# Three copies of the first y on two engines, and one softmax piece moved behind an output sum, in a fused dynamic convolution and squared-ReLU FFN

## Chip, cores and metric

One core of a Trainium2 chip. The metric is device time of one execution in microseconds (us). The program runs on one core, so there is no other core to compare with, and every profiled run here had a mean granted TensorE clock of 1.000. The "span" of a trace, from the first to the last instruction, is some 1.7 us shorter than the device time of the same execution (746.6 for 748.35).

## The reference

```python
# x: 8 x 4096 x 192, weight_gen: 8 x 4096 x 8 heads x 7 taps
w = softmax(weight_gen, axis=-1)
out[b, s, h, g] = sum over k of w[b, s, h, k] * x_pad[b, s + k, h, g]   # six zeros ahead of each sequence
h = np.maximum(out.reshape(32768, 192) @ w_in, 0.0)                     # 192 x 2048
return (h * h @ w_out).astype(np.float32)                               # 2048 x 192
```

## The kernel before

The tokens are cut into blocks: two of 512, then 31 of 1024. A block of 1024 has 16 units (the first two blocks have eight) and is followed, in the next block, by the eight parts of its second matmul. The prediction and the text below call each of these parts a quarter and count them from 1 to 8 in the block in which they run; the code counts two of them as one. A convolution of the next block stands near the end of every block. TensorE does the convolution as matmuls with banded matrices; VectorE builds the bands from the softmax rows.

The convolution writes PSUM tiles `yp`, and ScalarE copies them to `y`. For the first blocks, with 512 tokens, one tile holds all three chunks of 256 columns:

```python
def st_conv(j):
    th = BLOCKS[j][1] * TB // 2            # 256 columns for j == 0
    per = 1024 // th
    yps = [ps_h.tile([P, 2 * TB], f32, name="yp", tag="h") for _ in range(-(-NK // per))]
    # ... banded matmuls into yps ...
    for n, yp in enumerate(yps):
        k0, k1 = n * per, min((n + 1) * per, NK)
        nc.scalar.copy(
            out=y[:, k0:k1, 0:th],
            in_=yp[:, 0 : (k1 - k0) * th].rearrange("p (k c) -> p k c", c=th),
        )
```

A unit (`st_unit`, "u") is a set of matmuls into `h`, ScalarE's Relu of 1024 columns into `t` and VectorE's square into `g`. A quarter ("M") of a block of 1024 is 32 matmuls into two PSUM accumulators with one buffer each. Every second M ends with the output sum:

```python
def o_sum(j, qt, ccs, o):
    # ...
    nc.scalar.copy(out=o_sb, in_=o[0][:, c])
    if len(o) == 2:
        nc.vector.tensor_tensor(out=o_sb, in0=o[1][:, c], in1=o_sb, op=AluOp.add)
```

The next quarter into the same accumulators waits for that sum (in the trace of before once for long enough to be listed, 0.62 us). Softmax is done in parts and pieces: ScalarE takes the exponential of a piece ("E"), VectorE does the rest ("S"):

```python
def soft(s):
    lo, hi = next(s.softs)
    s.total(lo, hi)
    s.recip(lo, hi)
    s.scale(lo, hi, nc.vector)
    # ... after the last piece of a part: send the rows off by DMA
```

The order is written by hand for blocks 0 to 3 and from tables after that ("B": bands, "C": convolution, "L": load of raw weights):

```python
steady = "MuMuuu" * 3 + "MuuuMCu"
plans = {
    # ... blocks 0 to 2 ...
    3: "L5 L6 M S3 u u u M u u u u M u M B6 E4 u u u M M B7 u u S4 u E4 M u C M u",
}
TIMES = {(1, 0): ((3, 15), (4, 0)), (1, 1): ((4, 15), (5, 0)), ...}   # (block, unit) of each piece
us = {6: (7, 9)}.get(j, (5, 9) if small else (1, 5))                  # units ahead of which the bands stand
```

The softmax here doesn't subtract the row's maximum and nothing guards it: scores larger than these inputs give would overflow.

## Time and profile before

| | before |
|---|---|
| device time, median of 3 | 748.11 us (747.69 to 749.93) |
| span in the trace | 746.6 us |
| TensorE, VectorE, ScalarE busy | 99%, 83%, 84% |
| wait for the first y | 0.9 us, once |
| wait for an output sum | 0.6 us, once, near 78 us |

Busy shares say how near an engine is to full over the whole span; the two waits are what the change is aimed at. They add up to 0.2% of the time, so the question is one of tenths of a microsecond, read from the starts of instructions. The lines stand in the prediction below.

### The profile page before, as it was taken

What the parts mean: (1) busy time and instruction counts of PE and PEld (TensorE: products, weight loads), DVE (VectorE), ACT (ScalarE), POOL (GpSimd) and SP (SyncE); (2) the same over time, 40 slices, a digit from 0 to 9 for tenths busy, and PEclk for the clock granted to TensorE, in tenths of its full rate; (3) what the DMA queues carried; (4) which work ended last, traced back from release to release, by engine and by line L of the source; (5) the groups of instructions that cost most, each with busy time, mean ns of one, the idle gap of its engine ahead of it and who ended that gap; (6) DMA issues with size and microseconds to landing.
All of it is one profiled execution on the core that took longest, in us unless ns stands there. A gap on an engine that the chain in (4) does not pass through costs nothing.

```text
span 746.6 us, 33289 instructions
## 1 busy us (share of the span) xinstructions
PE 739.0 (99%) x15106; PEld 556.5 (75%) x15106; DVE 621.8 (83%) x1001; ACT 624.7 (84%) x755; POOL 88.8 (12%) x130
## 2 busy tenths in 40 slices
PE   8999999999999999999999999999999999999998
PEld 4767877877777777777777777787777777777787
DVE  5999998998889888888889888898888987677853
ACT  5998788888888888888888888888888888888874
POOL 7321220101101100011000110001100011001000
PEclk9999999999999999999999999999999999999999
DMA  8654454436554234644245542365441354441312
GB/s 223 112 106 109 80 101 85 100 70 139 94 118 79 75 57 80 140 79 73 45 74 139 102 65 53 51 139 108 59 80 48 57 108 80 60 73 51 51 46 65
DMA packets 122169, 64.81 MB, mean 87 GB/s; under 512 B 83849, under 2 KB 118636, under 8 KB 121516
## 3 DMA queue, kind: packets, MB, share of 16 engines
q1 hardware_dynamic: 77708, 45.66, 22.4%
q0 software_dynamic: 44176, 16.93, 20.5%
q8 instruction: 118, 1.93, 1.1%
q14 instruction: 23, 0.19, 0.1%
q10 hardware_dynamic: 144, 0.10, 0.0%
HBM read 48.61 MB, written 28.70 MB: 104 GB/s over the span
## 4 chain that ended last, share of the span: by engine, by line
PE 94%; DVE 2%; issue 1%; DMA 1%; ACT 1%; POOL 0%; DVEq 0%; ACTq 0%
PE o L475 45%; PE h L441 43%; PE yp L416 6%; DVE g L453 1%; DVE bd L348 1%; DMA wr<-v_first 0%; DMA wg<-in_weight_gen_dram 0%; POOL wr L330 0%; ACT t L450 0%; DVE v_first L239 0%; ACT ex L217 0%; DVE ssum L224 0%; DVE rcp L231 0%; DVE o_sb L491 0%; ACT y L427 0%
## 5 line engine op out<-in xcount | busy, mean ns | idle before, releaser
L450 ACT ACTIVATE t<-h 128x1024 f16<-128x1024 f32 x512 | 496.7, 1026 | 65.6 <-PE h L441 65.3
L453 DVE TENSOR_TENSOR g<-t 128x1024 f16<-128x1024 f16 x512 | 334.3, 687 | 100.5 <-ACT t L450 97.8
L475 PEld LDWEIGHTS <-g 64*128 64x128 f16 (+1 forms) x8032 | 352.3, 94 | 55.0 <-issue 4.8
L475 PE MATMUL o<-w_o,g 64*128 64x192 f16 (+1 forms) x8032 | 385.3, 243 | 0.9 <-DVE o_sb L491 0.6
L441 PE MATMUL h<-y,w_i 64*128 64x512 f16 (+1 forms) x3168 | 379.7, 370 | 2.2 <-ACT t L450 0.9
L441 PEld LDWEIGHTS <-w_i 64*128 64x128 f16 x3168 | 162.6, 94 | 117.2 <-issue 5.2
L348 DVE TENSOR_TENSOR bd<-wr,mask 128x4160 f16<-128x4160 f16 (+3 forms) x89 | 149.3, 1701 | 4.0 <-DMA wr<-v_first 4.0
L300 POOL DMA_DIRECT2D xt<-in_x_dram x62 | 51.2, 830 | 446.7 <-PE yp L416 423.7
L489 ACT COPY o_sb<-o 128x384 f32<-128x384 f32 x129 | 62.2, 482 | 33.8 <-PE o L475 33.8
L491 DVE TENSOR_TENSOR o_sb<-o,o_sb 128x384 f32<-128x384 f32 x123 | 68.2, 555 | 8.4 <-ACT o_sb L489 5.6
L427 ACT CAST y<-yp 128x1024 f16<-128x1024 f32 (+1 forms) x64 | 48.1, 803 | 14.5 <-PE yp L416 14.5
L416 PE MATMUL yp<-bd,xt 128*32 128x104 f16 (+8 forms) x3864 | 51.7, 208 | 0.3 <-DVE bd L348 0.2
L416 PEld LDWEIGHTS <-xt 128*32 128x32 f16 (+3 forms) x3864 | 46.2, 92 | 6.7 <-issue 6.2
L239 DVE TENSOR_TENSOR v_big<-ex,rcp 128x112 f16<-128x112 f32 (+1 forms) x136 | 27.3, 263 | 1.8 <-DMA vd<-v_big 0.6
L217 ACT ACTIVATE ex<-wg 128x448 f32<-128x448 f32 (+2 forms) x44 | 27.2, 618 | 1.8 <-DMA wg<-in_weight_gen_dram 1.8
L224 DVE TENSOR_REDUCE ssum<-ex 128x64 f32<-128x448 f32 (+2 forms) x44 | 26.1, 594 | 2.5 <-ACT ex L217 2.3
L231 DVE RECIPROCAL rcp<-ssum 128x64 f32<-128x64 f32 (+2 forms) x44 | 23.7, 539 | 1.5
L290 POOL DMA_DIRECT2D xt<-in_x_dram x7 | 3.8, 549 | 135.8 <-PE yp L416 135.8
L330 POOL DMA_DIRECT2D wr<-v_first x31 | 16.8, 561 | 16.3 <-DVE v_first L239 16.1
L539 PE MATMUL wp<-warm 128*128 128x512 f16 x39 | 11.4, 459 | 1.3 <-DVE warm L531 1.3
L539 PEld LDWEIGHTS <-warm 128*128 128x128 f16 x39 | 4.3, 114 | 7.6 <-issue 3.5
L239 DVE TENSOR_TENSOR v_first<-ex,rcp 128x112 f16<-128x112 f32 (+1 forms) x48 | 9.1, 255 | 0.3
(24 smaller groups left out, 28.2 us busy)
## 6 DMA issues: line engine op xcount, KB each, us to landing
out_dram<-o_sb SPq DMA_DIRECT2D x63, 384.0 KB, 3.0
xt<-in_x_dram POOLq DMA_DIRECT2D x42, 240.0 KB, 5.9
wg<-in_weight_gen_dram SPq DMA_DIRECT2D x4, 1064.0 KB, 8.3
xt<-in_x_dram POOLq DMA_DIRECT2D x20, 192.0 KB, 5.6
wr<-vd SPq DMA_DIRECT2D x38, 80.0 KB, 3.6
vd<-v_big SPq DMA_DIRECT2D x5, 512.0 KB, 5.5
wg<-in_weight_gen_dram SPq DMA_DIRECT2D x5, 392.0 KB
wg<-in_weight_gen_dram SPq DMA_DIRECT2D x3, 616.0 KB, 4.1
```

The source lines that it names most:

```text
L217: nc.scalar.activation(out=self.ex[:, lo:hi].rearrange("p r g k e -> p (r g) k e"), in_=self.wg[:, lo:hi].rearrange("p r (g e) k -> p (r g ...
L239: eng.tensor_tensor(out=bass.AP(tensor=v.tensor, offset=v.offset + lo * H * SL + lo % SL * 2 + g * SL * 2, ap=[list(v.ap[0]), [H * SL + 2, ...
L300: eng.dma_start(out=dst[:, first:last], in_=ap)
L348: nc.vector.tensor_tensor(out=bd_t[j][:, H * lo : H * (lo + len(tiles) * n)].rearrange("p (g m c) -> p g m c", g=shape[1], c=2 * SL), in0= ...
L416: nc.tensor.matmul(out=yps[k // per][p0 : p0 + m, col + a : col + b], lhsT=x_t[s][:, i, 32 * q : 32 * q + m], rhs=bd[:, h // 2, h % 2, a - ...
L427: nc.scalar.copy(out=y[:, k0:k1, 0:th], in_=yp[:, 0 : (k1 - k0) * th].rearrange("p (k c) -> p k c", c=th),)
L441: nc.tensor.matmul(out=h[:, half, jj * th : (jj + 1) * th], lhsT=w_in_chunk(u * per + jj, slot, half), rhs=y_t[j][r0 : r0 + RT, k, 0:th], ...
L450: nc.scalar.activation(out=t1, in_=h, func=ActF.Relu)
L453: nc.vector.tensor_tensor(out=g, in0=t1, in1=t1, op=AluOp.mult)
L475: nc.tensor.matmul(out=oo[:, cc * Dm : (cc + 1) * Dm], lhsT=g[r0 : r0 + n, cc * P : (cc + 1) * P], rhs=w_o[r0 : r0 + n, fc, :], start=(fc ...
L489: nc.scalar.copy(out=o_sb, in_=o[0][:, c])
L491: nc.vector.tensor_tensor(out=o_sb, in0=o[1][:, c], in1=o_sb, op=AluOp.add)
```

## The change

Its intent: the first copy of y lies between the first convolution and the first unit, with nothing else for TensorE to do; three copies on two engines could be done sooner than one of 768 columns. And near 78 us an output sum comes late because a softmax piece stands ahead of it on VectorE; the piece goes behind the last output sum of block 3. What followed it (the second piece of that part, and the bands that need its rows) moves later too.

```diff
@@ st_conv
-            nc.scalar.copy(
-                out=y[:, k0:k1, 0:th],
-                in_=yp[:, 0 : (k1 - k0) * th].rearrange("p (k c) -> p k c", c=th),
-            )
+            copies = ((k0, k1, nc.scalar.copy),)
+            if j == 0:
+                copies = ((0, 1, nc.scalar.copy),) + tuple(
+                    (k, k + 1, nc.vector.tensor_copy) for k in range(1, NK)
+                )
+            for a, b, copy in copies:
+                copy(
+                    out=y[:, a:b, 0:th],
+                    in_=yp[:, (a - k0) * th : (b - k0) * th].rearrange("p (k c) -> p k c", c=th),
+                )
@@ plans
-            3: "L5 L6 M S3 u u u M u u u u M u M B6 E4 u u u M M B7 u u S4 u E4 M u C M u",
+            3: "L5 L6 M S3 u u u M u u u u M u M B6 E4 u u u M M B7 u u u M u M C S4 u",
@@ TIMES
-            (1, 0): ((3, 15), (4, 0)),
+            (1, 0): ((3, 15), (4, 1)),
-            (1, 2): ((4, 1), (5, 1), (5, 15)),
+            (1, 2): ((4, 2), (5, 1), (5, 15)),
@@ exp_time
-            return j, {1: 0, 7: 3, 9: 4, 15: 8}[u]
+            return j, {1: 0, 2: 1, 7: 3, 9: 4, 15: 8}[u]
@@ bands
-            us = {6: (7, 9)}.get(j, (5, 9) if small else (1, 5))
+            us = {4: (7, 9), 6: (7, 9)}.get(j, (5, 9) if small else (1, 5))
```

In the prediction and below, part 1 is the first y, part 2 the end of block 3, part 3 the second softmax piece, part 4 the bands.

## The prediction

> **What bounds the kernel now.** I read the page's busy table first, then the list of waits of TensorE, then the timeline around each of those waits. The busy table says that TensorE is never free for long:
>
> ```profile
> PE 739.0 (99%) x15106; PEld 556.5 (75%) x15106; DVE 621.8 (83%) x1001; ACT 624.7 (84%) x755; POOL 88.8 (12%) x130
> ```
>
> TensorE is busy for 739.0 of 746.6 us, so everything that any change of waits could win is under 8 us, or 1%. VectorE and ScalarE are at 83% and 84%: close enough to full that work moved from one place to another in their queues can come late somewhere else. Of TensorE's waits, all under 2 us, three matter here:
>
> ```profile
> PE h L441 <- ACT t L450: 0.9, 1, 0.9
> PE h L441 <- ACT y L427: 0.9, 1, 0.9
> PE o L475 <- DVE o_sb L491: 0.6, 1, 0.6
> ```
>
> Columns: waiter, what it waited for, total us, times, longest. The second is the wait for the first y, which the first part of the change is aimed at. The third is the wait for an output sum, which the second part is aimed at. Here is the first, in the timeline (start us, us, engine, line, operation):
>
> ```profile
> 14.70 0.80 ACT L427 CAST y<-yp 128x768 f16<-128x768 f32 x1 [1.92 <-PE yp L416]
> ...
> 14.89 2.36 DVE L348 TENSOR_TENSOR bd<-wr,mask 128x3328 f16<-128x3328 f16 x2 [0.73 <-DMA wr<-v_first]
> ...
> 15.55 2.80 PE L441 MATMUL h<-y,w_i 64*128 64x256 f16 x48 [0.89 <-ACT y L427]
> ```
>
> The reader sees one ScalarE copy of 0.80 us between the convolution and the first unit, 0.05 us of signalling after it, and VectorE starting the bands of block 1 at 14.89. The other wait, on TensorE:
>
> ```profile
> 76.85 0.81 PE L441 MATMUL h<-y,w_i 64*128 64x512 f16 x6
> 77.57 0.24 PE L475 MATMUL o<-w_o,g 64*128 64x192 f16 x1
> 78.43 1.48 PE L475 MATMUL o<-w_o,g 64*128 64x192 f16 x31 [0.62 <-DVE o_sb L491]
> 79.68 0.87 PE L441 MATMUL h<-y,w_i 64*128 64x512 f16 x6
> ```
>
> and on VectorE, from block 3's end into block 4:
>
> ```profile
> 74.64 0.61 DVE L224 TENSOR_REDUCE ssum<-ex 128x64 f32<-128x448 f32 x1
> ...
> 75.87 0.83 DVE L239 TENSOR_TENSOR v_first<-ex,rcp 128x112 f16<-128x112 f32 x4
> 76.62 1.28 DVE L453 TENSOR_TENSOR g<-t 128x1024 f16<-128x1024 f16 x2
> 77.83 0.55 DVE L491 TENSOR_TENSOR o_sb<-o,o_sb 128x384 f32<-128x384 f32 x1
> ...
> 79.37 0.49 DVE L224 TENSOR_REDUCE ssum<-ex 128x48 f32<-128x336 f32 x1
> ...
> 84.88 2.69 DVE L453 TENSOR_TENSOR g<-t 128x1024 f16<-128x1024 f16 x4
> 87.59 0.56 DVE L491 TENSOR_TENSOR o_sb<-o,o_sb 128x384 f32<-128x384 f32 x1
> ```
>
> One piece of softmax (74.64 to 76.70) stands ahead of two squares and the output sum, the sum ends at 78.38, and the second matmul of the next quarter, which needs that accumulator, starts at 78.43. The true loss is read from starts: elsewhere in the timeline a unit is followed by a quarter after 0.65 us and a quarter by a unit after 1.32, so the unit at 79.68 should have come at 76.85 + 0.65 + 1.32 = 78.82. Loss: 0.86 us. From 79 to 720 us TensorE is busy for 640.6 of 641 us, so nothing after that is to be won.
>
> [...] for this question the starts of the matmul groups decide, and they repeat a block of 22.54 us over and over, so the pace between waits is set by TensorE's own work. [...] The first y has three chunks of 256 columns[...]. No trace of before shows two such readers, but the built order of the changed kernel does: VectorE's first copy waits for ScalarE's. [...] The trace has no VectorE copy out of PSUM; its output sum of 384 columns takes 555 ns[...]. [...] the trace has 1012, 810 and 593 ns for y copies of 1024, 768 and 512 columns, which makes 380 ns for 256 on its own straight line.
>
> **Part 1, the first y.** Removed: one ScalarE copy of 0.80 us. Added: one of 0.38 on ScalarE, two of 0.42 on VectorE. If all began at 14.70, the first unit could start at about 15.1, 0.4 us earlier. They do not[...]. ScalarE 14.70 to 15.08; VectorE's chunk 1 from 15.12 to 15.54; chunk 2 from 15.45 (successive VectorE instructions overlap by some 0.09 in the trace) to 15.87. The built order shows TensorE's waits: the first matmul on ScalarE, the second on chunk 1, the fifth on chunk 2. So matmul 2 starts near 15.59 (before: 15.55 + 0.06) and matmul 5 near 15.92, against 15.55 + 4 x 0.058 = 15.78. The remaining eight follow at the old pace. The first unit thus ends about 0.1 us later, not earlier. ScalarE then runs without a break worth naming from 16.41 to 27.2 us and TensorE waits for it (the 0.9 us at 21.05), so these 0.1 us pass on to the end. On VectorE the bands of block 1 start 0.9 us later, at 15.78; its two rests in 19.2 to 20.1 take up half, so the bands of block 2 end near 32.8 instead of 32.43, still ahead of their convolution at 33.13. Sum of part 1: +0.1 us.
>
> **Part 2, block 3's end.** The order of VectorE becomes: bands, four squares, output sum, softmax piece. The eighth quarter now stands ahead of the convolution, so its sum has 1.5 + 0.65 us of TensorE work over it before the next quarter needs the accumulator. ScalarE's copy (0.48) and the sum (0.55) fit in. The wait goes: -0.86 us.
>
> **Part 3, the second piece of that softmax part.** It moves from ahead of unit 0 of block 4 to ahead of unit 1. On VectorE it now stands between the sum of quarter 2 and that of quarter 4, where another part's piece (82.83 to 84.97) already stands. In the kernel before, VectorE worked from 82.36 to 87.57 without a rest (sum, piece, four squares), and the sum of quarter 4 began at 87.59, just when ScalarE's copy (87.08 to 87.56) was there. So there is no slack, and 1.72 us of softmax (79.37 to 81.09), about 1.64 of pitch, go in. In the clock of the kernel before, from quarter 1 on: sum of quarter 4 from about 87.50 + 1.64 = 89.14 to 89.70; quarter 5, which starts at 88.82, gets its second accumulator at 89.75. The unit behind it comes 1.25 us later (as 79.68 came after 78.43), at 91.00 instead of 90.14. Loss: +0.86 us. The wait has moved by two quarters. Where VectorE rested before, 78.38 to 78.76 and 81.09 to 81.65, it now only rests more.
>
> **Part 4, the bands two units later.** VectorE runs in order, so bands or squares first, the sum of quarter 6 comes after the same work: 5.2 us after that of quarter 4, and quarter 7 comes 5.23 us after quarter 5. No further wait, perhaps 0.05. The rows for these bands come by DMA from a piece now finished 3.6 us later; they had 7 us, the bands come 3.2 us later by order, and landing takes about 4: no wait. Their convolution is still 2 us away. 0.
>
> Sum: +0.1 - 0.86 + 0.86 + 0 = +0.1 us; 748.11 becomes 748.2.
>
> **Rivals.** *The change works as meant.* The wait is gone and VectorE catches up in time, because it has 0.8 us of gained rest ahead of quarter 2. For it: the author placed the pieces by hand and may have measured. Against it: that rest lies ahead of the sum of quarter 2, which no work can pass in an in-order queue. It would give 748.11 - 0.86 + 0.1 = 747.35; with part 1 in parallel as well, some 746.9. *VectorE's backlog costs more than one wait.* Two pieces side by side delay the squares as well, and quarter 7 or the bands' rows come late too. For it: VectorE's queue has no rest until 98 us. Against it: t has five buffers and the DMA margin above is about 3 us. It would give 749 to 749.3. *Part 1 gains.* If the wait on ScalarE cost nothing, 0.4 us: 747.7. Against it stands the built order.
>
> **Range and chances.** All of these lie between 746.9 and 749.3. Three runs of before spread over 747.69 to 749.93, so the median itself moves by some 0.3. Since the change was presumably kept for a reason, I lean a little to the first rival and say 748.0, range 747.0 to 749.1. To be 2% off would take 15 us, twice TensorE's whole idle time to gain, and a stall of a kind that nothing here shows to lose: 0.99 for within 2%.
>
> **What would show it.** In the profile of after: TensorE's wait for y should become waits on VectorE's copies, with the fifth matmul near 15.9, and ScalarE's first t at about 16.5 (16.41 before). The 0.62 us wait for the output sum near 78 should be gone, and a like wait of 0.6 to 0.9 us for an output sum should stand near 88.8, with two softmax pieces side by side on VectorE some 5 us earlier. No wait for bands near 98. I am wrong if no wait for an output sum remains in the list of waits (then the first rival holds), if VectorE's two copies start beside ScalarE's at 14.7, or if the first t comes earlier than 16.3.

Cut from the prediction is what it told of the hardware with no trace of this case to show it. The sum came to +0.1 - 0.86 + 0.86 + 0 = +0.1 us (748.2), and no term is taken out of it. But part 1's +0.1 has lost two of its grounds: where the 0.42 us for a VectorE copy came from, and why VectorE's copies should wait for ScalarE's (a reason that a run below refutes). What the trace of the changed kernel measures of both: the two copies took 411 and 424 ns, and VectorE idled 0.93 us and began 0.40 us after ScalarE. "Two such readers" are two engines that read one PSUM tile. That VectorE runs in order can be seen here: in the traces of before and after all its 1001 and 1003 instructions start in the order of the built program, compared by source line; and in before it idled 0.38 us ahead of the square at 78.76, with the softmax piece behind that square (79.37) not taken first, although the piece's exponential had ended at 74.10.

## The result

| | before | after |
|---|---|---|
| median of 4 runs | 747.93 us (747.69 to 749.93) | 747.76 us (747.40 to 747.86) |
| span in the trace | 746.6 us | 746.1 us |
| ratio after/before, 95% interval | | 0.9991 [0.9973, 1.0009] |

A ratio is the mean time of one kernel's fast runs over that of the other's fast runs of the same rounds, so it is not quite the ratio of the medians beside it. All runs of these two kernels were fast ones, and all kernels below gave the right result; of a kernel with one run (before_again, before_load, y_only_load, y_own_banks) the state is unknown.

The busy table of the changed kernel is that of before to within 0.7 us, except for the weight loads (PEld), which are 1.5 us longer:

```profile
PE 738.3 (99%) x15106; PEld 558.0 (75%) x15106; DVE 621.9 (83%) x1003; ACT 624.1 (84%) x755; POOL 88.9 (12%) x130
```

From its list of TensorE's waits (waiter, what it waited for, total us, times, longest):

```profile
PE o L482 <- DVE o_sb L498: 0.5, 1, 0.5
PE h L448 <- ACT y L434: 0.5, 1, 0.5
...
PE h L448 <- DVE y L434: 0.2, 1, 0.2
```

The wait for the first y is now in two pieces, on ScalarE and on VectorE, 0.7 us in all instead of 0.9. There is still one wait for an output sum. Where each stands, the timeline shows (start us, us, engine, line, operation, idle time before it and its releaser). First the start of the first unit:

```profile
15.11 0.37 ACT L434 CAST y<-yp 128x256 f16<-128x256 f32 x1 [1.94 <-PE yp L416]
15.51 0.75 DVE L434 CAST y<-yp 128x256 f16<-128x256 f32 x2 [0.93 <-ACT y L434]
...
15.99 1.47 PE L448 MATMUL h<-y,w_i 64*128 64x256 f16 x20 [0.19 <-DVE y L434]
...
16.97 1.02 ACT L457 ACTIVATE t<-h 128x1024 f16<-128x1024 f32 x1 [1.49 <-PE h L448]
```

VectorE had been idle for 0.93 us and still began 0.40 us after ScalarE, when ScalarE's copy had ended. So the copies stand one after the other. From the start of the first copy to the first `t` it is 16.97 - 15.11 = 1.86 us, against 16.41 - 14.70 = 1.71 before.

Next, the place of the old wait, TensorE and then VectorE:

```profile
78.11 1.48 PE L482 MATMUL o<-w_o,g 64*128 64x192 f16 x32
79.43 0.81 PE L448 MATMUL h<-y,w_i 64*128 64x512 f16 x6
```

```profile
76.54 0.56 DVE L498 TENSOR_TENSOR o_sb<-o,o_sb 128x384 f32<-128x384 f32 x1
77.02 0.61 DVE L224 TENSOR_REDUCE ssum<-ex 128x64 f32<-128x448 f32 x1
```

The sum ends at 77.10, the quarter that needs its accumulator starts at 78.11 and runs its 32 matmuls in one group. The unit behind it starts 1.32 us later, the undisturbed pitch. That wait is gone. Four quarters on, at quarter 5, TensorE:

```profile
88.57 0.24 PE L482 MATMUL o<-w_o,g 64*128 64x192 f16 x1
89.29 1.48 PE L482 MATMUL o<-w_o,g 64*128 64x192 f16 x31 [0.48 <-DVE o_sb L498]
90.55 0.87 PE L448 MATMUL h<-y,w_i 64*128 64x512 f16 x6
```

and VectorE ahead of it:

```profile
82.58 0.49 DVE L224 TENSOR_REDUCE ssum<-ex 128x48 f32<-128x336 f32 x1
...
84.23 0.68 DVE L460 TENSOR_TENSOR g<-t 128x1024 f16<-128x1024 f16 x1
84.83 0.61 DVE L224 TENSOR_REDUCE ssum<-ex 128x64 f32<-128x448 f32 x1
...
86.89 1.89 DVE L460 TENSOR_TENSOR g<-t 128x1024 f16<-128x1024 f16 x3
88.69 0.55 DVE L498 TENSOR_TENSOR o_sb<-o,o_sb 128x384 f32<-128x384 f32 x1
```

Two softmax pieces with one square between them push the output sum to 88.69 to 89.24, and the second matmul of the quarter starts at 89.29. The same wait, for the same kind of sum, eleven microseconds later. The unit behind it starts 90.55 - 88.57 = 1.98 us after the quarter instead of 1.32, so 0.66 us are lost. Before, 0.86 were lost at the old place.

Where did the 0.5 us of span between these two traces come from, then? By the starts of the first y copy, the first output matmul, and the convolutions used by blocks 3, 5 and the last block:

- The first y copy starts 0.41 us later (15.11 against 14.70). It comes 3.13 us after the first bands begin in both, and these, which wait for softmax rows by DMA (3.69 us idle ahead of them, 3.32 before), began 0.41 later (11.98 against 11.57) although the rows were sent at nearly the same time (8.31 against 8.27). Nothing in the change lies ahead of it in the program.
- From there to the first output matmul: 10.71 against 10.56, +0.15 us. This is part 1.
- From block 3's convolution to block 5's: 45.84 against 46.02, -0.18 us. These are parts 2 to 4.
- From block 5's convolution to the last: 609.81 against 610.55, -0.74 us, although the instructions and their order are the same.
- The rest, -0.14 us, lies in the other stretches.

So what the change did adds up to about zero, and the half microsecond is of another kind. That was to be tested.

### The profile page after: what moved, and what is told of

It is laid out like the page before. It is cut to its first block, busy times and chain, and to the rows that moved or that the text cites. A ratio compares the mean times of both kernels' runs of the same rounds, so it can differ in the third digit from the quotient of the medians.

```text
span 746.1 us, 33290 instructions
## 1 busy us (share of the span) xinstructions
PE 738.3 (99%) x15106; PEld 558.0 (75%) x15106; DVE 621.9 (83%) x1003; ACT 624.1 (84%) x755; POOL 88.9 (12%) x130
## 4 chain that ended last, share of the span: by engine, by line
PE 94%; DVE 3%; DMA 1%; ACT 1%; issue 1%; DVEq 0%; ACTq 0%
PE o L482 45%; PE h L448 43%; PE yp L416 6%; DVE bd L348 1%; DVE g L460 1%; DMA wr<-v_first 0%; DMA wg<-in_weight_gen_dram 0%; ACT t L457 0%; DVE v_first L239 0%; DVE ssum L224 0%; DVE rcp L231 0%; ACT ex L217 0%; DVE o_sb L498 0%; ACT y L434 0%; ACT o_sb L496 0%
```

## The experiments

Theory: part 1 costs 0.1 to 0.15 us because VectorE's copies must wait for ScalarE's. Part 2 removes a wait, and part 3 puts it back four quarters later because VectorE has a backlog with no slack there. Rivals: the second wait has another cause (ScalarE's copy, or something that the shorter first wait brings forward); part 1's loss is hidden further on; the difference between the two kernels is chance.

Twelve runs were made, four of them of a kernel that had run before, in three groups; each group ran on one chip and shared its runs of the kernel before. The medians of before were 748.68 us (747.44 to 749.81, 11 runs), 749.51 (747.72 to 750.95, 11) and 748.95 (748.46 to 749.70, 9). One table of the stretches that matter, from the traces, in us. "y" is the start of ScalarE's first y copy; the next three columns count from it, to the first `t`, to the second exponential on ScalarE and to the first output matmul; "3 to 5" is from block 3's convolution to block 5's, "5 to end" from there to the last convolution.

| kernel | group | y | to first t | to 2nd exp | to first output matmul | 3 to 5 | 5 to end |
|---|---|---|---|---|---|---|---|
| before | | 14.70 | 1.71 | 4.44 | 10.56 | 46.02 | 610.55 |
| after | | 15.11 | 1.86 | 4.59 | 10.71 | 45.84 | 609.81 |
| before_again | 1 | 14.34 | 1.72 | 4.69 | 10.80 | 46.01 | 610.68 |
| after_again | 1 | 15.07 | 1.86 | 4.59 | 10.73 | 45.80 | 610.75 |
| y_only | 1 | 15.27 | 1.86 | 4.59 | 10.73 | 46.01 | 610.58 |
| plan_only | 1 | 14.41 | 1.72 | 4.62 | 10.73 | 45.80 | 610.24 |
| piece_longer | 2 | 14.64 | 1.86 | 4.59 | 10.72 | 46.83 | 610.46 |
| piece_early | 2 | 14.65 | 1.72 | 4.73 | 10.83 | 45.70 | 610.41 |
| y_own_banks | 2 | 14.70 | 1.86 | 4.59 | 10.72 | 46.03 | 610.59 |
| y_two_tiles | 2 | 15.11 | 1.55 | 4.63 | 10.74 | 46.01 | 610.18 |
| before_load | 3 | 14.65 | 1.71 | 4.44 | 10.57 | 46.01 | 610.89 |
| y_only_load | 3 | 14.60 | 1.86 | 4.59 | 10.73 | 46.01 | 610.76 |
| both_mended_load | 3 | 14.96 | 1.56 | 4.29 | 10.41 | 45.75 | 610.01 |
| piece_early_again | 3 | 14.65 | 1.72 | 4.44 | 10.57 | 45.50 | 611.05 |

### before_again and after_again: how large is chance?

Both kernels unchanged, from fresh builds.

> The kernel before, once more. If the moments at which DMAs land set some of the differences between the two traces, its convolution of block 0 should end at another moment than 14.66 us by up to 0.4 us, and single blocks should again be 0.1 to 0.4 us longer than 22.54, but not the same ones. If instead those differences belong to the kernels, this trace repeats the first one within 0.05 us up to the convolution of block 6 and after it. Either way: the wait for an output sum near 78 us, 0.6 us in the list of waits, is there.

> The changed kernel, once more, over five rounds. My sum (part 1 +0.1, part 2 -0.86, part 3 +0.7 to +0.86) says 0.0 to -0.1 us against before, a ratio of 0.9998 to 1.0; a theory by which the change works as meant says -0.8 to -1.2 us, 0.9985 to 0.9990. In the trace: from the first copy of y to ScalarE's first t 1.86 us again, and the wait for an output sum near 89 us again.

Measured: before_again 748.09 us (one run, span 746.3); after_again 748.60 (748.32 to 748.79), ratio 0.9998 [0.9986, 1.0010], span 746.9. This time the changed kernel has the longer span. The two gains and losses of the change repeat (1.86 against 1.72; 45.80 against 46.01), the -0.74 us of the last stretch does not (610.75 against 610.68). Over all fourteen traces the same instructions from block 5's convolution to the last take between 609.81 and 611.05 us. A difference of 1.24 us in work that is the same drowns 0.2 us in end-to-end time: the stretches have to decide.

### y_only and plan_only: the two halves of the change

y_only is the kernel before with the `copies` lines of the diff alone. plan_only has the rest of the change and this in place of part 1:

```diff
-            if j == 0:
+            if False:
```

> Part 1 alone: the copies of the first y split, the rest as before. If VectorE's copies queue behind ScalarE's, the time from the start of ScalarE's first y copy to the start of its first t grows from 1.71 us to about 1.86, VectorE is told to wait for ScalarE, and the time is 0.1 to 0.2 us longer than before. If the split gains and the first trace only hid it in a later start, that stretch is near 1.3 us and the time 0.4 us shorter. The wait near 78 us for an output sum stays at 0.6.

> Parts 2 to 4 alone, the first y copied by ScalarE in one piece. If the wait only moves, the one near 78 us is gone, one of 0.4 to 0.7 us stands at quarter 5 of block 4 (near 88.5), from the convolution of block 3 to that of block 5 it is 0.1 to 0.3 us shorter than in before (46.02 us), and the time is 0.1 to 0.3 us shorter. If the wait near 89 us in the changed kernel came from part 1's delay of VectorE, it is absent here and the stretch is 0.8 us shorter.

Measured: y_only 750.34 us (748.93 to 751.34), ratio 1.0018 [1.0005, 1.0031]; plan_only 747.93 (747.01 to 749.24), ratio 0.9992 [0.9979, 1.0006]. The stretches add up: y_only has the 1.86 us of the change and the 46.01 of before, with the old wait of 0.62 us in its place; plan_only has the 1.72 of before and the 45.80 of the change, with the new wait of 0.47 us at 88.56. So part 1 is worth +0.15 us at the first `t`, and parts 2 to 4 are worth -0.2.

The 1.3 us (ratio 1.0018) by which y_only's mean is above that of before are more than its trace explains. Its first y copy started at 15.27, late because the first bands began at 12.14 instead of 11.2 to 11.6 as in the early executions. To see whether that belongs to the kernel, the same file ran again:

> Part 1 alone, as in y_only, run as it is a second time, beside before_load. It shows whether its late start (first y copy at 15.27 us, against 14.3 to 14.7 without the split) belongs to the kernel or to that execution, and whether the first output matmul comes 10.7 us after the first y copy again. If the split itself made the first loads land later, the first y copy is again at 15.1 or later; if it was chance, it may be anywhere from 14.3 to 15.3.

Measured: 748.71 us (one run; before in that group 748.95), first y copy at 14.60, and all other stretches as in y_only. (The label promises a load; the kernel is y_only unchanged.) So the kernel does not always start late. That the start is chance is not shown, though: in column "y" of the table the six traces without split copies start at 14.34 to 14.70 (mean 14.57), the eight with them at 14.60 to 15.27 (mean 14.93). If the split does move the start, part 1 costs more than the 0.15 us counted from the first copy. What made y_only's timed runs slow in group 1 stays open: its two traces, one of them of the fastest run, do not show it. Two of the six timed runs (751.34 and 750.46 us) had a granted clock of 0.998, but 750.55 and 750.23 us came at 1.000.

### piece_longer: is there slack on VectorE?

The changed kernel with the total and reciprocal of the moved second piece done twice, about 1 us more on VectorE, with the same result:

```diff
-            s.total(lo, hi)
-            s.recip(lo, hi)
+            for _ in range(2 if s is parts[4] and lo else 1):
+                s.total(lo, hi)
+                s.recip(lo, hi)
```

> The changed kernel with the second piece of the fifth softmax part made longer: its sum and its reciprocal are done twice (same results), 0.53 + 0.48 = 1.0 us more of VectorE between the output sums of quarters 2 and 4 of block 4. If the wait at quarter 5 is VectorE's backlog there, without slack, it grows by those 1.0 us, from 0.48 to near 1.5 in the list of waits, and the time by 1.0 us against the changed kernel (ratio to before near 1.001). If the wait has another cause (the DMAs of the rows, the accumulator's ScalarE copy), it stays at 0.5.

Measured: 749.39 us (748.86 to 750.17), ratio 1.0003 [0.9988, 1.0017]. On TensorE:

```profile
89.81 1.48 PE L482 MATMUL o<-w_o,g 64*128 64x192 f16 x31 [1.51 <-DVE o_sb L498]
91.07 0.87 PE L448 MATMUL h<-y,w_i 64*128 64x512 f16 x6
```

The wait grew from 0.48 to 1.51 us, by all that was added, and the stretch from 45.84 to 46.83. Had ScalarE's copy set the end of the wait, or had VectorE any rest there, part of the added microsecond would have vanished. The cause of the new wait is VectorE's backlog.

### piece_early: the second piece where it was

plan_only with part 3 undone: the second piece goes back ahead of unit 0 of block 4, its exponential just ahead of the convolution. The bands stay two units later.

```diff
-            3: "... B7 u u u M u M C S4 u",
+            3: "... B7 u u u M u M E4 C S4 u",
-            (1, 0): ((3, 15), (4, 1)),
+            (1, 0): ((3, 15), (4, 0)),
-            (1, 2): ((4, 2), (5, 1), (5, 15)),
+            (1, 2): ((4, 1), (5, 1), (5, 15)),
```

> Parts 2 and 4 without part 3: output sum of block 3 ahead of the first piece, the second piece ahead of unit 0 of block 4 as in before (its exponential ahead of the convolution), first y in one piece. VectorE then does the second piece in its rest ahead of the sum of quarter 2. My theory: no wait for an output sum, neither near 78 nor near 89 us; the convolution of block 3 to that of block 5 takes 46.02 - 0.86 = 45.2 us (before: 46.02, plan alone: 45.45), and the time is 0.7 to 0.9 us shorter than before, ratio 0.9989. The rival by which some wait must always remain in that stretch since VectorE is full says a wait of 0.3 to 0.5 us somewhere there, 45.5 us.

> The kernel piece_early once more. Again no wait for an output sum. Its first trace had, between the convolutions of block 3 and block 5, three longer steps of TensorE of 0.1 to 0.3 us that wait for no semaphore in the profile (0.6 us in sum), so the stretch was 45.70 instead of 45.16 us. If these belong to where the program's instructions lie, they come at the same matmuls again; if they are chance, they come elsewhere. Time: 0.7 to 0.9 us shorter than before, ratio 0.9989, as in the first run 0.9985.

Measured: piece_early 748.05 us (747.67 to 748.98), ratio 0.9985 [0.9971, 0.9998]; piece_early_again 748.31 (747.74 to 748.69), ratio 0.9991 [0.9977, 1.0004]. No wait for an output sum is left in the list of either, and none at quarter 5, which confirms that part 3 made that one. Yet the stretch from block 3 to block 5 came down to 45.70 and 45.50 us only. Without any loss it should have been 46.02 - 0.86 = 45.16. About 0.3 of the missing 0.34 to 0.54 us is the same in both, and in both_mended_load. On TensorE of piece_early_again:

```profile
93.20 1.85 PE L482 MATMUL o<-w_o,g 64*128 64x192 f16 x32
94.83 2.17 PE L448 MATMUL h<-y,w_i 64*128 64x512 f16 x18
```

The unit comes 1.63 us after the quarter, not 1.32, with no wait reported. On VectorE, just before:

```profile
87.94 0.69 DVE L460 TENSOR_TENSOR g<-t 128x1024 f16<-128x1024 f16 x1 [0.64 <-ACT t L457]
88.85 0.69 DVE L460 TENSOR_TENSOR g<-t 128x1024 f16<-128x1024 f16 x1 [0.22 <-ACT t L457]
89.46 2.39 DVE L348 TENSOR_TENSOR bd<-wr,mask 128x832 f16<-128x832 f16 x2
...
92.97 0.55 DVE L498 TENSOR_TENSOR o_sb<-o,o_sb 128x384 f32<-128x384 f32 x1
```

Now VectorE is early: it rests for 0.64 and 0.22 us for lack of `t` while the bands stand two units further back in its queue, does the bands after that, and the next sum (92.97 to 93.52) comes after the quarter has begun at 93.20. The quarter's first matmul does not need that accumulator. Its second does, and a view of TensorE from 93.46 to 93.6 us alone shows its start:

```profile
93.57 0.26 PE L482 MATMUL o<-w_o,g 64*128 64x192 f16 x2
```

That is 0.05 us after the sum's end. So a wait of 0.3 us for an output sum is left, at quarter 7. The first matmul's modelled end (93.20 + 0.24 = 93.44) covers all of it but 0.13 us, and the list of waits has no row for that. Why the sum is late is a reading: the later bands, which cost nothing beside a VectorE that is late, cost 0.3 us beside one that is early. It was not tested: the kernel with the bands back at units 5 and 9 and no late piece was not run. The first piece_early also took 0.19 us too long for the quarter at 55.17, and both_mended_load 0.24 for the one at 55.06; piece_early_again did not. That is unexplained.

### y_own_banks and y_two_tiles: half or tile?

The prediction put VectorE's wait down to the place of chunks 0 and 1 in one half of the PSUM tile (its columns 0 to 511). No trace had shown that, so it was tested. The label and the expectation call such a half of 512 columns a bank, as `banks` in the kernel's code does. y_own_banks is y_only with chunks 1 and 2 moved to the second half of the same PSUM tile:

```diff
             col = th * (k % per) - base
+            if j == 0 and k:
+                col += TB - th
```

(and the copies read from there). y_two_tiles is y_only with chunk 0 in a PSUM tile of its own:

```diff
-            ps_h.tile([P, 2 * TB], f32, name="yp", tag="h") for _ in range(-(-NK // per))
+            ps_h.tile([P, 2 * TB], f32, name="yp", tag="h")
+            for _ in range(2 if j == 0 else -(-NK // per))
-            col = th * (k % per) - base
+            n, first = (int(k > 0), int(k > 0)) if j == 0 else (k // per, k - k % per)
+            col = th * (k - first) - base
```

> Part 1 alone, one PSUM tile, but with chunk 0 in its first bank and chunks 1 and 2 in its second. If the shared bank is why VectorE waits, the wait goes; the built order says that it does not, so the wait comes from the shared tile: VectorE's first copy starts after ScalarE's copy has ended (0.4 us after its start), and the stretch from ScalarE's y copy to its first t is 1.86 us as in the change.

> Part 1 alone, the same three copies, but chunk 0 in one PSUM tile and chunks 1 and 2 in another; the rest as before. The built order shows VectorE waiting for TensorE only. If the order of the two copies was what cost part 1 its gain, VectorE's first copy starts together with ScalarE's, and from the start of ScalarE's y copy to its first t it takes about 1.4 us (before 1.71, change 1.86). The time, the rest being equal, is 0.3 us shorter than before and 0.45 shorter than part 1 alone. If the gain is eaten by ScalarE later, TensorE's wait for t near 21 us grows by the same amount.

Measured: y_own_banks 748.91 us (one run); y_two_tiles 748.72 (748.65 to 749.55), ratio 0.9994 [0.9981, 1.0007]. The timeline of y_own_banks:

```profile
14.70 0.37 ACT L436 CAST y<-yp 128x256 f16<-128x256 f32 x1 [1.92 <-PE yp L418]
15.10 0.76 DVE L436 CAST y<-yp 128x256 f16<-128x256 f32 x2 [0.93 <-ACT y L436]
```

and that of y_two_tiles:

```profile
15.11 0.37 ACT L436 CAST y<-yp 128x256 f16<-128x256 f32 x1 [1.82 <-PE yp L418]
15.21 0.76 DVE L436 CAST y<-yp 128x256 f16<-128x256 f32 x2 [0.54 <-PE yp L418]
...
19.74 0.93 ACT L217 ACTIVATE ex<-wg 128x784 f32<-128x784 f32 x1 [0.23 <-DMA wg<-in_weight_gen_dram]
```

With the chunks in different halves VectorE still waits for ScalarE (0.93 us idle, released by its copy, 0.40 us after it). With different tiles it does not (0.10 us after it, released by TensorE). So the wait belongs to the shared tile of the program: in these builds the two engines' copies from one PSUM tile come one after the other, from one half of it and from two (0.40 us apart in both). The prediction's step was right in its size and wrong in its reason.

y_two_tiles brings the first `t` 0.31 us earlier than the change and 0.16 earlier than before (1.55 us after the first copy, where about 1.4 had been expected). Its first copy needs only the tile of chunk 0 and starts 0.16 us after the start of the convolution's last matmul, for 0.24 in the others; counted from that matmul the gains are 0.39 and 0.25 us. Nothing of that reaches the first output matmul (10.74): the second exponential now waits 0.23 us for its weights, which come by a DMA issued at 14.52, 5.22 us before it starts, so the gain is eaten four microseconds later.

### before_load and both_mended_load: can the gain be kept?

before_load is the kernel before with that load issued ahead of two others:

```diff
-        cross_w_in(1)
         s1.load(nc.sync)
+        cross_w_in(1)
```

both_mended_load has this, y_two_tiles and piece_early together.

> The kernel before, with the load of the second softmax part's weights one place earlier in its DMA queue (ahead of the crossing of the second half of w_in, so near 11.5 us instead of 14.0). If in the traces so far the second exponential, near 19 us, waits for these weights to land some 5.1 us after their issue, it now comes straight behind the third t: 4.44 us after the start of the first y copy (before, in three of four traces, 4.6 to 4.7), and the first output matmul 10.56 us after it (10.7 to 10.8). If the weights are not the limit there, these stay at 4.6 to 4.7 and 10.7 to 10.8.

> The changed kernel mended at three places: chunk 0 of the first y in a PSUM tile of its own, the second piece of the fifth softmax part ahead of unit 0 of block 4 (as in piece_early), and the second part's weights loaded earlier (as in before_load). No wait for an output sum in blocks 3 and 4 (-0.79 us); from the first y copy to the first output matmul 10.40 us (before 10.7 to 10.8: -0.3 to -0.4). Sum -1.1 to -1.2 us against before, ratio 0.9985. If the early load disturbs the rows of blocks 0 and 1, the first y copy comes later by some tenths and the gain shrinks to 0.8.

Measured: before_load 748.73 us (one run); both_mended_load 747.84 (747.31 to 748.92), ratio 0.9989 [0.9976, 1.0002], span 746.0. In both_mended_load the second exponential waits for nothing:

```profile
16.52 2.86 ACT L459 ACTIVATE t<-h 128x1024 f16<-128x1024 f32 x3 [1.18 <-PE h L450]
...
19.25 0.95 ACT L217 ACTIVATE ex<-wg 128x784 f32<-128x784 f32 x1
```

It comes 4.29 us after the first copy and the first output matmul 10.41 us after it, 0.15 less than the best of the kernel before (0.25 counted from the convolution's last matmul). So with the tiles apart and the load earlier, the gain reached TensorE in this one trace. The ratio of 0.9985 that had been expected was missed: the 0.3 us at quarter 7 are lost here too. There is a consequence for part 1: with the load where it was, the kernels with one copy have their second exponential at 4.44 us in two traces of five and at 4.62 to 4.73 in three, those with split copies in one tile at 4.59 in all six; part 1's 0.15 us therefore reach the first output matmul in some executions and are covered in others, by the load as the author reads it. before_load shows 4.44, but that is one trace, so for the kernel before the load as the cause is consistent and not shown.

No version beat both kernels clearly. piece_early and both_mended_load have means 0.15% and 0.11% under that of before, with intervals that only just leave out or take in 1; the second run of piece_early has 0.09%, and its interval takes in 1.

## Why the prediction was right

748.0 us was predicted, within 747.0 and 749.1; 747.76 was measured. That the two lie 0.24 us apart is luck: the working gave 748.2, the step from there to 748.0 leaned to a rival that fell, and the median of the kernel before moved between 747.93 and 749.51 us from group to group. What can be judged is the steps:

- *What bounds the kernel.* Right. TensorE stayed at 99%, and no kernel moved by more than 0.2%. But "nothing after that is to be won", from 640.6 us busy of 641, does not follow from busy time: in piece_early_again a loss of 0.31 us at 93.20 shows as 0.13 us of idle time, and the rest of it as a busy TensorE.
- *Part 1, +0.1 us.* Right in size: +0.15 at the first `t` in six traces of split copies in one tile. VectorE's copies took 411 and 424 ns where 420 had been put, ScalarE's 372 for 380, and the second matmul started 0.88 us after the first copy began (15.99 - 15.11) where 0.89 had been reckoned (15.59 - 14.70). The separate wait of the fifth matmul does not show: twenty matmuls run on from 15.99 in one row. The reason was wrong: the shared tile makes VectorE wait, with chunks 0 and 1 in one half of it (0.93 us idle, in the changed kernel) and in two (0.93, y_own_banks). Not foreseen was that block 1's convolution now waits 0.26 us, at 19.16, for VectorE's cast of x, which begins 3.34 us after the first copy instead of 2.47 (before_again and plan_only, with one copy, have such a wait too). It costs nothing: TensorE's next wait for `t` ends at 21.61, only the 0.15 us later than before, counted from the first copy. That the loss passes on to the end is only partly so, since in three of five traces with one copy the second exponential is as late without it (4.62 to 4.73 us).
- *Part 2, -0.86 us.* Right: the wait near 78 is gone and the pitch there is back at 1.32.
- *Part 3, +0.86 us.* The wait is where it was foretold, between the first and second matmul of quarter 5 (four quarters on; the prediction's "two" counts as the code does), with two pieces on VectorE ahead of it; piece_longer and piece_early show the cause from both sides. The size was off: a wait of 0.48 us was listed where 0.6 to 0.9 had been foretold, and 0.66 was lost by the starts where 0.86 had been reckoned. The term that was mis-sized is "there is no slack". In the kernel before, the four squares at 84.88 took 2.69 us as one row; another row of four, in the same trace, took 2.49:

```profile
90.36 2.49 DVE L453 TENSOR_TENSOR g<-t 128x1024 f16<-128x1024 f16 x4
```

  So 0.2 us of waiting were hidden inside the first row. Views of the kernel before, of ScalarE from 85.6 to 86.9 us and of VectorE from 86.8 to 87.6 us, show where:

```profile
85.82 1.02 ACT L450 ACTIVATE t<-h 128x1024 f16<-128x1024 f32 x1 [0.41 <-PE h L441]
```

```profile
86.88 0.69 DVE L453 TENSOR_TENSOR g<-t 128x1024 f16<-128x1024 f16 x1
```

  The last square began at 86.88, just after its `t` was done at 86.84; squares without a wait start 0.60 us apart, and it came 0.79 after the one before it. In the changed kernel, from the sum of quarter 2 to that of quarter 4 VectorE needs 88.69 - 82.11 = 6.58 us, where the working has 89.14 - 82.36 = 6.78. Those 0.2 us are the whole gain of parts 2 to 4.
- *Part 4, 0.* Right in the change, where no further wait came at quarter 7. Two estimates were off for the changed kernel, without effect: counted from the start of quarter 2 (80.08 and 80.33) the bands came 2.55 us later instead of 3.2, and the rows, for which about 4 us had been put, landed after 1.7 to 2.2 us in the changed kernel (those issued from 80 to 90 us; 3.6 to 4.3 in the kernel before). It is not a free move in general: where the second piece is not late, these bands are followed by a step of 1.63 us instead of 1.32.
- *Sum.* +0.15 - 0.86 + 0.66 + 0 = -0.05 us, for +0.1 predicted. Both are far below what end-to-end times can tell: the -0.5 us of span between the first two traces is 0.41 of late rows against 0.74 of chance in the identical part.
- *The rivals.* "Works as meant" (747.35) fell with the wait at 89.29. "Backlog costs more than one wait" fell: one wait, 0.66. "Part 1 gains" fell for the change, but its 0.4 us against before are there in part: 0.16 once the tiles are apart (0.25 counted from the convolution's last matmul), and only with an earlier load did they reach the first output matmul.

## What to carry to other kernels

When a piece of work is moved behind a deadline on an engine that starts its instructions in program order, as VectorE did here (1001 of 1001 in before), find the next deadline of the same engine and add up everything between the two; a move only wins what rest lies in between, here 0.2 us of 0.86. Splitting a PSUM read between two engines needed a tile for each in these builds, or the second waited for the first (its copy began 0.40 us after the other's with one tile, 0.10 with two); and a gain at the start has to be followed to the next load that lands, which may take it back (here a wait of 0.23 us for weights). Where a kernel's unchanged part varies by more than the effect sought, time that effect between two instructions next to it and repeat the trace, instead of trusting a run's time.
